# Decoding the second MLP's weights one matrix further ahead, with second buffers

## The chip, the cores and the metric

One core of a Trainium2 chip runs the whole program. The metric is the time of the device in microseconds for one execution, as a median over runs. The engines are TensorE (PE in the profile), VectorE (DVE), ScalarE (ACT), GpSimd (POOL), and SyncE (SP), which issues the DMAs. Each engine works through its own list of instructions strictly in order, so an instruction that waits holds up all that stands behind it on its engine.

## The reference

```python
def _moe_ref(x, w_gate, w_val, w_out):
    gate = 1.0 / (1.0 + np.exp(-(x @ w_gate)))
    val = x @ w_val
    return (gate * val @ w_out).astype(np.float32)

def _moe2_ref(x, w_a, w_b, w_out):
    a = x @ w_a
    b = x @ w_b
    return (a * b @ w_out).astype(np.float32)

def reference(**kwargs):
    attn_out = _attn_ref(**attn_kwargs)      # 4 x 8 heads, 576 positions, 64 wide, window of 64
    B, H, S, D = attn_out.shape
    x = np.ascontiguousarray(attn_out.transpose(0, 2, 1, 3)).reshape(B * S, H * D)
    x = _moe_ref(x=x, **moe_kwargs)
    return _moe2_ref(x=x, **moe2_kwargs)
```

The 2304 tokens are 512 wide. Both MLPs have 1536 hidden columns, and all six weight matrices arrive as 64-bit floats.

## The kernel before

The hidden columns of each MLP are cut into 12 chunks of 128 (NF = 12). The code counts the chunks of both MLPs in one row: F = 0 to 11 is the first MLP, F = 12 to 23 the second. A chunk has three matrices of 128 x 512 elements, a, b and o. Each is **decoded** on the chip, since the engines know no 64-bit floats: a matrix comes in as two 32-bit words for each element (tile st_a, st_b or st_o, by DMA), and becomes a high part and a low part for PE.

Decoding one matrix has two halves. decode_words (L371) builds the words: ACT makes low (L375) and ex (L378), DVE makes wi in two instructions (L381, L384), and POOL adds low to wi (L388). decode_pair (L392 on) is the split: DVE multiplies ex by wi (L394), ACT writes the high part (L400), and the low part is a subtraction (L403) that runs on DVE for a and b and on POOL for the second MLP's o. SP then saves the pair to DRAM (tiles ka, kb, ko). For the second MLP there are besides four sums and differences of halves of a and b, made by combinations: on POOL s (L447), on ACT the high part wq (L449), on POOL the low part of wq (L450), and a save by SP. There is one buffer for low, one for wi, two for ex.

In the second MLP, each chunk's up-projections are a **quad** (q0 to q11 below, one for each of F = 12 to 23): instead of eight block products seven are made, in the order 1, 5, 6, 2, 7, 4, 3, each of six matmuls, into three banks (qa, qb, qc). ACT copies intermediate sums out of a bank (r1, r2, r3, L845; pool "rs"), DVE adds them up (g0, g1 and qc, L848), multiplies (qa and qc, L858), ACT and DVE split the product into the hidden tile hh, hl (L477, L479), and PE multiplies that by the chunk's o into accq (L964). The result of the accumulation is added to resf (L968). While quad k is worked on, a later chunk is decoded, by calls of step_decode between pieces of PE's work. For the first MLP in this stretch the same is done with plain products (gps, vps, L468), with hr and hh made from them (L488, L477).

The order of instructions on each engine is fixed when the program is built: a scheduler, with its own cost model, places the work in the order in which the Python code emits it and as its buffers allow. In `decode`, one call of step_decode did one whole matrix, words and split together, and the loads of the next chunk came at the end of a chunk. In time: to about 225 us runs the attention with the first chunks of the first MLP, to 350 us the rest of it, from 350 to 560 us the quads of the second MLP's front blocks with the decoding of its chunks, from 640 us on all weights are fetched back ready-made from DRAM.

Of the kernel before, what the change touches and what calls it, by code (L numbers as in the profile page):

```python
# [21 lines left out]
def tile_window_attention_gated_mlps(ctx, tc, q, k, v, w1g, w1v, w1o, w2a, w2b, w2o, out):  # L22
# [348 lines left out]
    def decode_words(F, i, nm):  # L371
        st = staged.pop((F, nm))
        w0, w1 = st[:, :, 0], st[:, :, 1]
        low = dec.tile([P, DM], I32, tag="low", name="low")
        nc.scalar.activation(out=low, in_=w0.bitcast(U32), func=AF.Copy, scale=2.0 ** -29)  # L375
        yield
        ex = dec.tile([P, DM], F32, tag="ex", bufs=2, name="ex")
        nc.scalar.activation(out=ex, in_=w1.bitcast(F32), func=AF.Abs)  # L378
        yield
        wi = dec.tile([P, DM], I32, tag="wi", name="wi")  # L380
        nc.vector.tensor_scalar(  # L381
# [34 lines left out]

    def decode(F):
        for i, nm in enumerate("abo"):
            if nm not in parts.get(F, {}):
                whole(decode_words(F, i, nm))  # L420
                whole(decode_pair(F, i, nm))
                save(F, nm, pairs.pop((F, nm)))
                yield
                if F >= NF and nm == "b":
                    got = parts[F]
                    for n, t in combinations(got, full.pop((F, "a")), full.pop((F, "b"))):
                        nc.sync.dma_start(out=kept_q[F - NF][:, n], in_=t.bitcast(F32))
                    yield
        ready[F] = parts[F]

# [9 lines left out]
    def combinations(got, a, b):  # L440
# [3 lines left out]

        def combined(nm, x, y, op):
            s = late["sts"].tile([P, CH], F32, tag="s", name=f"s{nm}")
            nc.gpsimd.tensor_tensor(out=s, in0=x, in1=y, op=op)  # L447
            t = late["wq"].tile([P, 2, CH], F32R, tag="wq", name=f"wq{nm}")
            nc.scalar.activation(out=t[:, 0], in_=s, func=AF.Copy)  # L449
            nc.gpsimd.tensor_tensor(out=t[:, 1], in0=s, in1=t[:, 0].bitcast(F32), op=ALU.subtract)  # L450
            got[nm] = (t[:, 0], t[:, 1])
            return s, t

        s1, t5 = combined(5, b1, b2, ALU.add)
        s2, t6 = combined(6, s1, a1, ALU.subtract)
        _, t7 = combined(7, a1, b1, ALU.subtract)
        _, t3 = combined(3, a2, s2, ALU.subtract)
        return tuple(enumerate((t5, t6, t7, t3)))

# [182 lines left out]

    nload, ndec, dec_it, limit = [0], [0], [None], [NF - 1]

    def step_decode(turn):

        if dec_it[0] is None:
            F = ndec[0]
            if F >= NW or F > limit[0] or (F > G and last_use.get(F - G - 1, -1) >= turn):
                return False  # L650
            if nload[0] <= F:
                load_weights(F)
                nload[0] = F + 1
            dec_it[0] = decode(F)
            ndec[0] += 1
        if next(dec_it[0], "done") == "done":
            dec_it[0] = None
            F = ndec[0]
            if F < NW and nload[0] <= F:
                load_weights(F)  # L660
                nload[0] = F + 1
        return True
# [137 lines left out]
    def fetch(F, whole):  # L800
# [15 lines left out]
        else:  # L816
            f = got["f"].bitcast(F32)
            combinations(got, f[:, 0], f[:, 1])
        return got
# [220 lines left out]
    for F in range(DECODED):  # L1040
        ready[F] = parts[F]
    ndec[0] = nload[0] = DECODED
    done.update([*group_of, *BACK[:BEHIND]])

    for n, (group, fcs) in enumerate(plan):
# [6 lines left out]
        if n == SPAN.stop:  # L1052
# [3 lines left out]
            attend(steps=100)  # L1056
            next_part(early, (("op6", 1), ("hs", 1), ("wq", 8), ("sts", 3), ("rs", 3)), middle)
            limit[0] = NF + 1
# [246 lines left out]
```

## Time and profile before

| | us |
|---|---|
| median of 3 runs | 968.96 (966.82 to 969.8) |
| profiled execution, its own time | 969.65 |
| its span in the profile | 967.5 |
| PE busy | 931.7 (96%) |
| DVE busy | 687.1 (71%) |
| ACT busy | 482.1 (50%) |
| POOL busy | 360.4 (37%) |

The span is the stretch of the profiled execution from the first to the last instruction; 2.15 us of its time lie outside. Busy times are over the whole span, and the work isn't spread evenly: POOL has nothing to do in the last third, and 20 of every 25 us in some stretches of the second MLP's decoding. The mean clock granted to PE was 0.993 of full speed.

### The profile page before, as it was taken

The numbers are of one execution on the slowest core, as the hardware profiler recorded it, in microseconds if no ns is written. First come the engines' busy times: TensorE is split into PE (matmuls) and PEld (weight loads), VectorE is DVE, ScalarE is ACT, GpSimd is POOL, SyncE is SP. The second block draws the span as 40 slices with busy tenths as digits, with TensorE's granted clock in tenths as the row PEclk, the third lists the DMA queues.
The fourth block names the chain that finished last, engine by engine and source line by source line (L and its number), as shares of the span: only waits on it lengthen the run. The fifth ranks groups of instructions, "written<-read, shape, count | busy, mean of one in ns | idle before, by whom it ended". The sixth has DMA issues, their size and how long they took to land.

```text
span 967.5 us, 15682 instructions
## 1 busy us (share of the span) xinstructions
PE 931.7 (96%) x5504; PEld 776.6 (80%) x5504; DVE 687.1 (71%) x1339; ACT 482.1 (50%) x1063; POOL 360.4 (37%) x357
## 2 busy tenths in 40 slices
PE   7899999999799998998999998999999999999998
PEld 6798887887688886877887886788888888888886
DVE  6997877786653489878788866778888673344545
ACT  7887554576654365665556433664454233311111
POOL 4543223345422385686568518643440000000000
PEclk9999999999999999999999999999999999999999
DMA  8996698998763174767567547345455675554322
GB/s 212 246 246 194 215 342 305 314 302 269 249 210 110 70 249 149 254 231 248 196 214 261 210 150 262 111 159 169 141 174 197 217 255 159 164 172 129 101 66 87
DMA packets 146846, 193.69 MB, mean 200 GB/s; under 512 B 63825, under 2 KB 99153, under 8 KB 146769
## 3 DMA queue, kind: packets, MB, share of 16 engines
q1 hardware_dynamic: 146768, 192.71, 61.5%
q8 instruction: 43, 0.70, 0.3%
q14 instruction: 35, 0.28, 0.1%
HBM read 118.75 MB, written 69.47 MB: 195 GB/s over the span
## 4 chain that ended last, share of the span: by engine, by line
PE 68%; POOL 10%; DVE 9%; DMA 6%; issue 3%; ACT 3%; POOLq 0%; SPq 0%; DVEq 0%; ACTq 0%
PE qa L826 15%; PE accq L964 12%; PE qb L826 8%; PE gps L468 7%; PE vps L468 7%; PE accm L569 5%; PE qc L826 4%; POOL s L447 3%; POOL wi L388 3%; PE accy L927 3%; POOL wq L450 2%; PE accx L927 2%; DMA kf<-ex 2%; PE xps L228 2%; DMA wf<-kf 1%
## 5 line engine op out<-in xcount | busy, mean ns | idle before, releaser
L388 POOL TENSOR_TENSOR wi<-wi,low 128x512 int32<-128x512 int32 x72 | 101.8, 1413 | 136.3 <-DVE wi L384 99.3
L826 PE MATMUL qa<-op,wq 128*128 128x512 f32 x432 | 113.1, 390 | 1.5 <-ACT op L730 0.9
L826 PE MATMUL qb<-op,wq 128*128 128x512 f32 x432 | 111.5, 390 | 0.1
L468 PE MATMUL vps<-xh,wb 128*128 128x256 f32 (+1 forms) x392 | 106.9, 342 | 3.3 <-ACT hr L488 3.3
L845 ACT ACTIVATE r<-qa 128x512 f32<-128x512 f32 x108 | 62.6, 594 | 89.6 <-PE qa L826 88.1
L450 POOL TENSOR_TENSOR wq<-s,wq 128x256 fp32r<-128x256 f32 x96 | 88.4, 929 | 50.2 <-ACT wq L449 49.9
L468 PE MATMUL gps<-xh,wa 128*128 128x256 f32 (+1 forms) x392 | 105.7, 340 | 0.2 <-DVE hl L479 0.2
L826 PEld LDWEIGHTS qa<-op,wq 128*128 128x128 f32 x432 | 80.9, 188 | 19.4 <-ACT op L730 1.4
L826 PEld LDWEIGHTS qb<-op,wq 128*128 128x128 f32 x432 | 81.0, 188 | 17.4 <-DVE qc L848 0.5
L569 PE MATMUL accm<-hh,wo 128*128 128x512 f32 (+1 forms) x296 | 86.3, 359 | 4.2 <-DVE gacc L546 3.6
L394 DVE SCALAR_TENSOR_TENSOR ex<-ex,wi 128x512 f32<-128x512 f32 x72 | 58.2, 809 | 30.5 <-POOL wi L388 21.1
L468 PEld LDWEIGHTS vps<-xh,wb 128*128 128x128 f32 x392 | 70.8, 195 | 11.0 <-ACT hr L488 3.5
L468 PEld LDWEIGHTS gps<-xh,wa 128*128 128x128 f32 x392 | 70.0, 193 | 8.9 <-DVE hl L479 1.3
L964 PE MATMUL accq<-wo,h 128*128 128x512 f32 (+1 forms) x300 | 71.6, 382 | 1.8 <-DVE resf L968 1.7
L468 PE MATMUL gps<-xl,wa 128*128 128x256 f32 (+1 forms) x196 | 66.5, 339 | 0.6 <-DVE xl L237 0.6
L468 PE MATMUL vps<-xl,wb 128*128 128x256 f32 (+1 forms) x196 | 66.7, 340 | 0.0
L477 ACT ACTIVATE hh<-qa 128x512 fp32r<-128x512 f32 x36 | 21.5, 598 | 90.1 <-DVE qa L858 61.2
L964 PEld LDWEIGHTS accq<-wo,h 128*128 128x128 f32 x300 | 54.9, 188 | 13.6 <-DVE resf L968 2.3
L569 PEld LDWEIGHTS accm<-hh,wo 128*128 128x128 f32 x296 | 52.6, 189 | 13.5 <-DVE gacc L546 3.4
L964 PE MATMUL accq<-wo,hh 128*128 128x512 f32 x184 | 56.3, 397 | 5.8 <-ACT hh L477 5.6
L189 ACT ACTIVATE pr<-pr,stat 128x128 f32<-128x128 f32 x144 | 54.1, 391 | 12.3 <-DVE stat L183 11.9
L210 POOL TENSOR_TENSOR pr<-pr,stat 128x512 f32<-128x512 f32 x34 | 38.1, 1122 | 55.0 <-DVE stat L208 36.7
(177 smaller groups left out, 2125.7 us busy)
## 6 DMA issues: line engine op xcount, KB each, us to landing
wo<-ko SPq DMA_DIRECT2D x27, 512.0 KB, 4.1
wa<-ka SPq DMA_DIRECT2D x27, 512.0 KB, 4.4
st_o<-in_moe_w_out_dram SPq DMA_DIRECT2D x24, 512.0 KB, 5.0
ka<-wa SPq DMA_DIRECT2D x24, 512.0 KB, 4.9
kb<-wb SPq DMA_DIRECT2D x24, 512.0 KB, 4.6
ko<-wo SPq DMA_DIRECT2D x24, 512.0 KB, 4.3
kq<-wq SPq DMA_DIRECT2D x48, 256.0 KB, 3.5
wq<-kq SPq DMA_DIRECT2D x48, 256.0 KB, 3.1
```

The lines of the kernel that those rows point to most:

```text
L189: nc.scalar.activation(out=pr[e][:, j, :], in_=pr[e][:, j, :], func=AF.Exp, bias=nmax[:, e, j:j + 1], scale=-1.0, accum_out=None if t in O ...
L210: (nc.vector if t in OTHERS["norm"] else nc.gpsimd).tensor_tensor(out=pr[e], in0=pr[e], in1=den[:, e].unsqueeze(2).to_broadcast([P, NP, P] ...
L388: nc.gpsimd.tensor_tensor(out=wi, in0=wi, in1=low, op=ALU.add)
L394: nc.vector.scalar_tensor_tensor(out=wf, in0=wf, scalar=SMALLEST, in1=wi.bitcast(F32), op0=ALU.is_ge, op1=ALU.mult)
L447: nc.gpsimd.tensor_tensor(out=s, in0=x, in1=y, op=op)
L450: nc.gpsimd.tensor_tensor(out=t[:, 1], in0=s, in1=t[:, 0].bitcast(F32), op=ALU.subtract)
L468: nc.tensor.matmul(ps, lhsT=a[:, c * P:(c + 1) * P], rhs=b[:, c, :], start=(n == 0), stop=(n == 3 * NP - 1))
L569: nc.tensor.matmul(ps[:, m], lhsT=a[:, sl], rhs=b, start=k == 0, stop=k == total - 1)
L826: nc.tensor.matmul(ps, lhsT=a[:, c * P:(c + 1) * P], rhs=b[:, c, :], start=first and n == 0, stop=n == 5, skip_group_check=True,)
L845: nc.scalar.activation(out=r[n], in_=ps, func=AF.Copy)
L927: nc.tensor.matmul(bank[k], lhsT=a[n][i][:, sl], rhs=b[n][j], start=start and m == 0, stop=m == 2, skip_group_check=True,)
L964: nc.tensor.matmul(ps, lhsT=a, rhs=b, start=n == 0, stop=n == len(pairs) - 1)
```

## The change

The generator `decode`, which did matrix after matrix, goes. `begin_matrix` now issues the words of the next matrix and then at once the load of the same matrix of the next chunk, and step_decode does the split of the oldest matrix whose words are there. From F = 14 on (NF + 2) it first calls begin_matrix once more, so that the words of one further matrix stand ahead of the split. From F = 15 on, wi takes turns between its old buffer and a second one in a new pool "dec", and the ex of an o matrix gets a buffer of its own there, so that the two old ones are left to a and b. To make room, pool "rs" has two buffers instead of three. The four combinations of a chunk, once one step, are two steps of two; a first-MLP chunk takes three steps instead of four. What is computed and the number of instructions stay the same.

```diff
     def decode_words(F, i, nm):
         st = staged.pop((F, nm))
         w0, w1 = st[:, :, 0], st[:, :, 1]
+        k = 3 * F + i if F > NF + 2 else 0
         low = dec.tile([P, DM], I32, tag="low", name="low")
...
-        ex = dec.tile([P, DM], F32, tag="ex", bufs=2, name="ex")
+        ex = late["dec"].tile([P, DM], F32, tag="ex", name="ex") if k % 3 == 2 else dec.tile([P, DM], F32, tag="ex", bufs=2, name="ex")
...
-        wi = dec.tile([P, DM], I32, tag="wi", name="wi")
+        wi = (late["dec"] if k % 2 else dec).tile([P, DM], I32, tag="wi", name="wi")
...
-    def decode(F):
-        for i, nm in enumerate("abo"):
-            if nm not in parts.get(F, {}):
-                whole(decode_words(F, i, nm))
-                whole(decode_pair(F, i, nm))
-                save(F, nm, pairs.pop((F, nm)))
-                yield
-                if F >= NF and nm == "b":
-                    got = parts[F]
-                    for n, t in combinations(got, full.pop((F, "a")), full.pop((F, "b"))):
-                        nc.sync.dma_start(out=kept_q[F - NF][:, n], in_=t.bitcast(F32))
-                    yield
-        ready[F] = parts[F]
+    def combining(F):
+        got = combinations(parts[F], full.pop((F, "a")), full.pop((F, "b")))
+        for half in range(2):
+            for n, t in islice(got, 2):
+                nc.sync.dma_start(out=kept_q[F - NF][:, n], in_=t.bitcast(F32))
+            yield
...
+    def begin_matrix():
+        if begun[0] == 0:
+            load_weights(DECODED)
+        if begun[0] < len(order):
+            F, i, nm = m = order[begun[0]]
+            begun[0] += 1
+            whole(decode_words(*m))
+            pending.append(m)
+            if F + 1 < NW:
+                load_matrix(F + 1, nm)
 
     def step_decode(turn):
...
+        if combined_by:
+            if next(combined_by[0], combined_by) is not combined_by:
+                return True
+            combined_by.pop()
+        if not pending:
+            begin_matrix()
+        if not pending:
+            return False
+        F, i, nm = m = pending[0]
+        if F > limit[0] or (F > G and last_use.get(F - G - 1, -1) >= turn):
+            return False
+        if F >= NF + 2:
+            begin_matrix()
+        pending.pop(0)
+        whole(decode_pair(*m))
+        save(F, nm, pairs.pop((F, nm)))
+        if nm == "o":
+            ready[F] = parts[F]
+        elif nm == "b" and F >= NF:
+            combined_by.append(combining(F))
         return True
...
-            next_part(early, (("op6", 1), ("hs", 1), ("wq", 8), ("sts", 3), ("rs", 3)), middle)
+            next_part(early, (("op6", 1), ("hs", 1), ("wq", 8), ("sts", 3), ("rs", 2), ("dec", 1)), middle)
```

The order of instructions is the same on every engine up to about 225 us, and again once the front blocks' quads are done. Between, three places are shown. In the changed file the lines have moved by a few (L394 is L395 there, L848 is L861, L858 is L871, L388 is L389, L450 is L444, L447 is L441).

**ACT, in the last first-MLP chunks (about 262 us).** kt is a copy for the attention, ex and low are decoding words (ex_4355, now ex_4186, those of a later a matrix), hr is the copy of a product of the first MLP, which PE's next products in that bank wait for. Before:

```order
L118 ACTIVATE pt14_0_3498<-tps14_0_3493 128x512
L153 ACTIVATE kt17_3769<-kt16_3514 128x4x64
L378 ACTIVATE ex_4355<-st_a_4233 128x512
L488 ACTIVATE hr_3812<-gps_3786 128x256
L375 ACTIVATE low_4366<-st_b_4235 128x512
```

and now:

```order
L118 ACTIVATE kt16_3520<-kps16_3515 128x4x128
L401 ACTIVATE wo_3927<-ex_3918 128x512
L153 ACTIVATE kt17_3771<-kt16_3520 128x4x64
L483 ACTIVATE hr_3814<-gps_3788 128x256
L379 ACTIVATE ex_4186<-st_a_4033 128x512
L376 ACTIVATE low_4371<-st_b_4074 128x512
```

The copy hr, which stood behind the words ex, stands ahead of them.

**DVE, at quad q3 (about 430 to 438 us).** Here qc, qa and g belong to q3 (qa_5418 before, qa_5431 now, is the product that hh of q3 is split from); xacc is a sum of the accumulation's results; wi, ex and wb are decoding. Before, these stand behind the words of chunk 17's o matrix (wi_5513) and chunk 18's a (wi_5665):

```order
L403 TENSOR_TENSOR wb_5457<-ex_5450,wb_5457 128x512
L593 TENSOR_TENSOR xacc0_4918<-acc1_5384,xacc0_4918 128x512
L394 SCALAR_TENSOR_TENSOR ex_5511<-ex_5511,wi_5513 128x512
L381 TENSOR_SCALAR wi_5665<-st_a_5533 128x512
L384 SCALAR_TENSOR_TENSOR wi_5665<-st_a_5533,wi_5665 128x512
L858 TENSOR_TENSOR qa_5418<-qa_5418,g0_5416 128x512
L848 TENSOR_TENSOR g1_5417<-qb_5419,r2_5467 128x512
```

and now, with chunk 18's b (wi_5678) and o (wi_5707) and chunk 19's a (wi_5821):

```order
L385 SCALAR_TENSOR_TENSOR wi_5678<-st_b_5450,wi_5678 128x512
L588 TENSOR_TENSOR xacc0_4935<-acc0_5387,xacc0_4935 128x512
L588 TENSOR_TENSOR xacc0_4935<-acc1_5388,xacc0_4935 128x512
L395 SCALAR_TENSOR_TENSOR ex_5676<-ex_5676,wi_5678 128x512
L382 TENSOR_SCALAR wi_5821<-st_a_5545 128x512
L871 TENSOR_TENSOR qa_5431<-qa_5431,g0_5429 128x512
L385 SCALAR_TENSOR_TENSOR wi_5821<-st_a_5545,wi_5821 128x512
L404 TENSOR_TENSOR wb_5714<-ex_5676,wb_5714 128x512
L395 SCALAR_TENSOR_TENSOR ex_5705<-ex_5705,wi_5707 128x512
L861 TENSOR_TENSOR g1_5430<-qb_5432,r2_5484 128x512
```

The same product qa stands behind work for matrices that are two to three further on, and g1 behind three decoding instructions of its own.

**POOL, at the same quad.** The product qa of q3 above stands on DVE behind a multiplication L394 (now L395) that reads the wi which POOL adds up: wi_5513 before, wi_5678 now. POOL's rows up to that addition and on, before:

```order
L447 TENSOR_TENSOR s7_5479<-ex_5431,ex_5450 128x256
L450 TENSOR_TENSOR wq5_5471<-s5_5469,wq5_5471 128x256
L388 TENSOR_TENSOR wi_5513<-wi_5513,low_5509 128x512
L450 TENSOR_TENSOR wq6_5476<-s6_5474,wq6_5476 128x256
L450 TENSOR_TENSOR wq7_5481<-s7_5479,wq7_5481 128x256
L447 TENSOR_TENSOR s3_5484<-ex_5431,s6_5474 128x256
```

and now:

```order
L441 TENSOR_TENSOR s7_5514<-ex_5405,ex_5444 128x256
L441 TENSOR_TENSOR s3_5520<-ex_5405,s6_5492 128x256
L444 TENSOR_TENSOR wq6_5494<-s6_5492,wq6_5494 128x256
L404 TENSOR_TENSOR wo_5414<-ex_5291,wo_5414 128x512
L444 TENSOR_TENSOR wq7_5516<-s7_5514,wq7_5516 128x256
L404 TENSOR_TENSOR wo_5548<-ex_5465,wo_5548 128x512
L444 TENSOR_TENSOR wq3_5522<-s3_5520,wq3_5522 128x256
L389 TENSOR_TENSOR wi_5678<-wi_5678,low_5674 128x512
L389 TENSOR_TENSOR wi_5707<-wi_5707,low_5703 128x512
```

Before it was POOL's row number 186 of the whole program, now it is number 193: seven more of POOL's instructions (three wq, one s, one wo, two wi) stand ahead of it.

## Rows read from the trace of the kernel before

**Rows 1.** Windows: us; busy PE, PEld, DVE, ACT, POOL (instructions); clock, DMA, GB/s.

```profile
350.00:375.00 25.00, 22.12 (x109) 18.23 (x108) 24.46 (x32) 14.26 (x26) 14.71 (x12) 0.93 0.51 179
375.00:437.00 62.00, 57.03 (x266) 45.82 (x264) 49.51 (x70) 41.01 (x80) 50.47 (x46) 1.00 0.68 231
425.00:525.00 100.00, 94.82 (x425) 78.48 (x424) 82.12 (x124) 54.84 (x103) 69.16 (x66) 0.97 0.67 227
700.00:725.00 25.00, 25.00 (x112) 20.63 (x111) 20.87 (x34) 12.37 (x25) 10.34 (x14) 1.00 0.55 178
```

**Rows 2.** ACT's timeline, 255 to 270 us.

```profile
262.19 0.40 ACT L153 ACTIVATE kt<-kt 128x256 f32<-128x256 f32 x1
264.19 0.67 ACT L378 ACTIVATE ex<-st_a 128x512 f32<-128x512 f32 x1 [1.60 <-DVE wo L403]
264.77 0.37 ACT L488 ACTIVATE hr<-gps 128x256 f32<-128x256 f32 x1
```

**Rows 3.** PE's timeline, 257 to 272 us.

```profile
265.19 0.58 PE L468 MATMUL vps<-xh,wb 128*128 128x256 f32 x1 [3.29 <-ACT hr L488]
```

**Rows 4.** PE's timeline, 366 to 384 us.

```profile
378.83 1.43 PE L826 MATMUL qa<-op,wb 128*128 128x512 f32 x5 [0.47 <-DVE op L736]
```

**Rows 5.** DVE's timeline, 429 to 444 us.

```profile
430.16 0.68 DVE L403 TENSOR_TENSOR wb<-ex,wb 128x512 fp32r<-128x512 f32 x1
...
433.42 1.22 DVE L394 SCALAR_TENSOR_TENSOR ex<-ex,wi 128x512 f32<-128x512 f32 x1 [1.98 <-POOL wi L388]
...
436.56 0.68 DVE L858 TENSOR_TENSOR qa<-qa,g 128x512 f32<-128x512 f32 x1
```

**Rows 6.** PE's timeline, 429 to 445 us.

```profile
433.76 1.07 PE L826 MATMUL qa<-op,wq 128*128 128x512 f32 x4
437.93 1.20 PE L964 MATMUL accq<-wo,hh 128*128 128x512 f32 x4 [3.11 <-ACT hh L477]
```

**Rows 7.** Chain of waits, 400 to 800 us: start, length, engine, group.

```profile
439.13 2.40 PE gps L468 x12
...
443.95 1.42 PE gps L468 x12
...
449.56 1.36 PE accq L964 x6
...
510.46 2.60 PE accq L964 x6
```

**Rows 8.** DVE's timeline, 503 to 516 us.

```profile
504.89 0.69 DVE L394 SCALAR_TENSOR_TENSOR ex<-ex,wi 128x512 f32<-128x512 f32 x1 [0.27 <-POOL wi L388]
...
508.25 0.69 DVE L858 TENSOR_TENSOR qa<-qa,g 128x512 f32<-128x512 f32 x1
```

**Rows 9.** PE's timeline, 503 to 516 us.

```profile
510.46 1.75 PE L964 MATMUL accq<-wo,hh 128*128 128x512 f32 x4 [1.87 <-ACT hh L477]
```

**Rows 10.** Groups by form, 335 to 600 us, POOL.

```profile
L450 POOL TENSOR_TENSOR wq<-s,wq 128x256 fp32r<-128x256 f32 x58 | 56.4, 986 | 2.2 <-ACT wq L449 2.1
L388 POOL TENSOR_TENSOR wi<-wi,low 128x512 int32<-128x512 int32 x33 | 47.1, 1429 | 38.6 <-DVE wi L384 36.2 <-ACT hr L492 2.3
...
L403 POOL TENSOR_TENSOR wo<-ex,wo 128x512 fp32r<-128x512 f32 x12 | 18.7, 1561 | 10.7 <-ACT wo L400 10.7
```

**Rows 11.** Waits that end in 375 to 437 us: total, times, longest.

```profile
POOL wi L388 <- DVE wi L384: 15.6, 3, 9.5
...
POOL s L447 <- DVE ex L394: 3.2, 4, 0.8
```

**Rows 12.** ACT's timeline, 520 to 533 us.

```profile
526.23 0.59 ACT L845 ACTIVATE r<-qa 128x512 f32<-128x512 f32 x1
```

**Rows 13.** DVE's timeline, 522 to 533 us.

```profile
529.75 0.68 DVE L848 TENSOR_TENSOR g<-qb,r 128x512 f32<-128x512 f32 x1
```

**Rows 14.** POOL's timeline, 410 to 416 us.

```profile
412.70 1.25 POOL L447 TENSOR_TENSOR s<-s,ex 128x256 f32<-128x256 f32 x1
```

**Rows 15.** DVE's timeline, 410 to 416 us.

```profile
413.28 1.23 DVE L403 TENSOR_TENSOR wb<-ex,wb 128x512 fp32r<-128x512 f32 x1
```

More of the change, by code (lines that the diff above doesn't have):

```diff
@@ L443, in combinations, with combined @@
         (a1, a2), (b1, b2) = ((f[:, 0:CH], f[:, CH:]) for f in (a, b))
-        def combined(nm, x, y, op):
+        def combined(n, nm, x, y, op):
             s = late["sts"].tile([P, CH], F32, tag="s", name=f"s{nm}")
@@ L451, in combined @@
             got[nm] = (t[:, 0], t[:, 1])
[L452 to L458, printed above, removed]
+            return s, (n, t)
+        s1, t = combined(0, 5, b1, b2, ALU.add)
+        yield t
+        s2, t = combined(1, 6, s1, a1, ALU.subtract)
+        yield t
+        yield combined(2, 7, a1, b1, ALU.subtract)[1]
+        yield combined(3, 3, a2, s2, ALU.subtract)[1]
     def product(ps, w, x):
@@ L641, in tile_window_attention_gated_mlps @@
     NW = 2 * NF
-    nload, ndec, dec_it, limit = [0], [0], [None], [NF - 1]
-    def step_decode(turn):
[L647 to L661, printed above, removed]
+    limit = [NF - 1]
+    order = [(F, i, nm) for F in range(DECODED, NW) for i, nm in enumerate("abo")]
+    begun, pending, combined_by = [0], [], []
+    def begin_matrix():
[8 more added lines that the diff above has]
+                load_matrix(F + 1, nm)
+    def step_decode(turn):
+        if combined_by:
[18 more added lines that the diff above has]
+            combined_by.append(combining(F))
         return True
@@ L817, in fetch @@
             f = got["f"].bitcast(F32)
-            combinations(got, f[:, 0], f[:, 1])
+            *_, = combinations(got, f[:, 0], f[:, 1])
         return got
@@ L1041, in tile_window_attention_gated_mlps @@
         ready[F] = parts[F]
-    ndec[0] = nload[0] = DECODED
     done.update([*group_of, *BACK[:BEHIND]])
```

## The prediction

> **What bounds the kernel now.** I read the windows first, to see which engine is full in which stage. From 640 us on PE is: 25.00 us busy of 25, at full clock, in 700 to 725 [rows 1]. All of the decoding is over by then, so nothing that this change does can shorten that part; it only starts earlier or later. The change has to earn its time between 225 and 560 us. There PE is nearly full too, 57.03 of 62 us from 375 to 437 and 94.82 of 100 us from 425 to 525 [rows 1]. So about 5 us can be won in each of these stretches at the most, and only where PE stands still. I went from there to PE's timeline and looked for its longest idle times and what ended them. Three are large enough to matter: 3.29 us before 265.19, which the copy hr on ACT ended [rows 3], 3.11 us before 437.93 and 1.87 us before 510.46, both ended by hh of a quad on ACT [rows 6, 9]. Last I followed each of the three back on the engine that was late, with the timelines of ACT and DVE, and set beside it what stands there in the changed order.
>
> The sum goes against the profiled execution's own 969.65 us. The median of the runs is 0.7 us lower, and I take that off at the end.
>
> **ACT at 262 us.** The kt copy ends at 262.59. Behind it stood the words ex<-st_a, which waited until 264.19 for a buffer, and only behind these the hr that PE waited for, at 264.77 [rows 2]. With hr ahead of ex it can start at 262.59, since the product it copies was finished before PE went idle at 261.90 (265.19 less 3.29). That is 264.77 - 262.59 = **2.2 us** won. The ex that is moved back loses nothing, as its buffer came free only at 264.19. Neither end is far: 0 if PE's head start is lost in the next stretch, where DVE is busy 24.46 of 25 us [rows 1], and 3.3 if the matmuls behind the gap keep their speed too.
>
> **DVE between 363 and 380 us.** Here DVE is the full engine, and the order now puts one pair of word instructions of chunk 15 in front of the differences that q0's operand op is made from. PE already waits 0.47 us for such an op at 378.83 [rows 4]. Such a pair takes at most 1.9 us, the time between L394's end at 434.64 and qa's start at 436.56, with POOL busy beside it [rows 5]. It lies between 0 and 1.9; I take **1.0 us lost**.
>
> **DVE and POOL at quad q3.** PE is done with q3's products at 434.83, and hh is late by 3.11 us [rows 6]. It is late since qa (L858) starts on DVE only at 436.56, behind L394, L381 and L384 of the decoding, and L394 had stood 1.98 us waiting for POOL's addition [rows 5]. In the changed order qa stands behind L395 and L382, one instruction less, which by these rows lets POOL's addition end 1.1 to 2.0 us later without harm (3.14 us from L394's start to qa's before; 1.22 us and a word instruction now). But the addition that L395 needs is seven POOL instructions later. By their means these are three wq at 0.99, one s taken like a wq, one wo at 1.56 and two wi at 1.43, 8.4 us [rows 10]. So POOL has to do 6.4 to 7.3 us of work in time in which it used to stand, only for qa to be where it was. It has that time: 62 - 50.47 = 11.5 us idle from 375 to 437 [rows 1]. Of this, 6.1 us (15.6 less the 9.5 that lie before 375) it waited for DVE's wi, and 3.2 us for ex [rows 11]. These are the two waits that words one step ahead and a second wi take away, 9.3 us together. That leaves 9.3 - 6.4 = 2.9 down to 9.3 - 7.3 = 2.0 us by which qa comes earlier; I take **2.5 us** of the 3.11. What is late next is the same qa, by 0.6 us.
>
> With PE's idle time goes slow running behind it: twelve gps take 2.40 us right after the wait and 1.42 us five us later [rows 7], 1.0 us more, at a lower granted clock. With most of the wait gone I count **0.8 us** of that.
>
> **DVE at quad q7.** The same picture at 508.25: qa stands behind an L394 that began at 504.89 and three more decoding instructions, 3.4 us in all [rows 8], and PE waits 1.87 us for hh [rows 9]. The six accq behind take 2.60 us where six take 1.36 elsewhere [rows 7]. The work is the same at each quad, and by q7 the decoding has had four more chunks to get ahead, so I count both, 1.8 and 1.2, **3.0 us**.
>
> **Buffers "rs", two for three.** r1 and r3 now share a buffer, and r2 of the next quad has to wait until g1 of this one is added. In the trace r2 of a quad starts at 526.23, and the g1 that would have to be done first ends at 530.43, 4.2 us later [rows 12, 13], the largest such lag I found. PE needs r2 copied before product 7; what lies between is product 2 at least, six matmuls like the six of 1.36 us [rows 7], at the most two sums of accq of the same length besides. So 0.1 to 2.8 us at a quad can stand open, and the order has g1 behind three decoding instructions. I take the middle at one quad, **1.4 us lost**.
>
> **The rest costs nothing that I can find.** The loads st move ahead of some saves on SP, and start earlier than before; the words are needed no sooner than before. Steps of three instead of four in the first MLP move decoding earlier, into a stretch where the gap at 262 us is the largest. The combinations in two halves are the same instructions.
>
> The sum: -2.2 + 1.0 - 2.5 - 0.8 - 3.0 + 1.4 = -6.1, so 963.5 us on the profiled execution's scale and **962.8** as a median.
>
> **A rule that speaks against it.** POOL's s at 412.70 took 1.25 us and DVE's wb at 413.28 took 1.23 us [rows 14, 15], while the same wb takes 0.68 us at 430.16 [rows 5]: the two engines hold each other up. The Trainium skill says why ("SBUF — State Buffer", section "SBUF: two separate sides"): GpSimd shares a pair of ports with VectorE's operations that read two SBUF inputs, and whoever has it has it for its whole instruction. The trace agrees, 1.23 being 0.68 and most of another instruction. By that rule part of POOL's idle time is not there to be had, and the sum would be that of the second rival, 966.4.
>
> **Rivals.**
>
> *POOL can't make good the seven instructions (slower).* The mechanism is the in-order queue of DVE: qa waits behind L395, L395 for POOL. For it speaks that POOL is already the busiest of the three helpers there, 50.47 of 62 us [rows 1]; against it that 9.3 us of its idle time have just the causes that are taken away [rows 11]. If none of the idle time is recovered, qa is 6.4 us later instead of 2.5 earlier, nothing comes back at q7 either, and the sum is -2.2 + 1.0 + 6.4 + 1.4 = +6.6, or 976 us. It decides when POOL recovers less than about 6 of its 11.5 us: then q3 gives nothing back; below 4 us it costs 2.4 or more and eats the gain at 262 us.
>
> *DVE and POOL in each other's way (no change).* A chunk takes 18.1 us (510.46 - 437.93 over four quads) [rows 6, 9]. DVE's decoding instructions with two inputs are eight in it, at 0.68 us 5.4 us, 30 us in the 100 from 425 to 525, and POOL is busy 69.16 [rows 1, 5]: 99 of 100 us, if none of POOL's busy time is waiting. Some of it is, as at 412.70. Then only a third of the 8.3 us at q3 and q7 comes back and the sum is -2.2 + 1.0 - 2.8 + 1.4 = -2.6, 966.4 us as a median.
>
> *The ring of two.* If four quads stand open by 2.1 us each, it costs 8.4 for 1.4 us: -6.1 + 7.0 = +0.9, about 970 us.
>
> **How the numbers follow.** A measurement of this kernel can tell 0.3%, 2.9 us, from no change. I give the forecast 0.56, with its own range of 958 to 966: down to -3.3 - 3.1 - 1.0 - 3.0 = -10.4 where nothing is lost and the clock is kept, up to -3. The slow POOL has 0.16, the two engines in each other's way 0.18, the ring 0.10. Most of the forecast and some of the second rival are faster: 0.57. The rest of that rival and most of the ring are the same: 0.24. The slow POOL and the worst of the ring are slower: 0.19. The range from 955 to 971.5 leaves out the worse half of the slow POOL and little else; its lower end is the -10.4 less the 2.9 us that PE stands idle from 350 to 375 [rows 1], which I counted at nothing.
>
> **What would show it.** Right: hr on ACT directly after kt at about 262.6; PE's wait for hh at q3 under 1 us, and none at q7; POOL's waits for DVE's wi gone from 375 to 437 and its busy time there near 60 of 62 us. Wrong: DVE's L395 waiting for POOL with a qa behind it, for several us; PE waiting for r at product 7 of many quads; a new wait of PE between 365 and 380 for op.

## The result: 977.0 us for 968.7, slower by 0.75%

The changed kernel took 977.01 us (median of 4 runs, 975.53 to 977.40), the kernel before beside it 968.67 us. The ratio is 1.0075, with a 95% interval of 1.0052 to 1.0098: slower, by 8.3 us. The prediction was 962.8 us, in a range of 955 to 971.5.

The head of the page of the profile after:

```profile
span 974.8 us, 15689 instructions
...
PE 931.6 (96%) x5504; PEld 774.5 (79%) x5504; DVE 701.3 (72%) x1339; ACT 480.8 (49%) x1063; POOL 358.9 (37%) x357
```

PE did the same work in the same busy time (931.7 us before), and the span is 7.3 us longer: PE stands still for longer. DVE is busy 14.2 us longer than before (687.1) with the same 1339 instructions. POOL is not (360.4 before). So DVE's own instructions have become slower. The windows, with the columns of [rows 1]:

```profile
350.00:375.00 25.00, 21.42 (x110) 17.23 (x111) 24.39 (x31) 14.40 (x25) 13.83 (x10) 1.00 0.46 161
375.00:437.00 62.00, 54.08 (x246) 43.12 (x244) 56.04 (x69) 41.83 (x81) 54.23 (x48) 0.97 0.74 248
425.00:525.00 100.00, 93.55 (x421) 76.01 (x419) 86.26 (x118) 54.34 (x104) 66.44 (x65) 0.98 0.66 223
700.00:725.00 25.00, 25.00 (x112) 20.62 (x111) 21.28 (x35) 12.19 (x24) 10.73 (x15) 1.00 0.59 189
```

From 375 to 437 us DVE is busy 56.04 us where it was 49.51, with one instruction fewer, and PE 54.08 where it was 57.03 [rows 1]. The back part is as before, PE full.

PE's 5504 matmuls are the same in both kernels, so the place of the loss can be read from rows at which PE has the same amount of work behind it (starts in us):

| PE's row | before | after | later by |
|---|---|---|---|
| vps<-xl,wb | 340.17 | 338.92 | -1.25 |
| qa<-op,wb, at q0 | 378.83 | 378.45 | -0.38 |
| gps<-xh,wa, ahead of q2 | 401.83 | 407.01 | 5.18 |
| qa<-op,wb, at q3 | 429.22 | 434.39 | 5.17 |
| vps<-xl,wb, behind q3 | 442.72 | 448.07 | 5.35 |
| qa<-op,wa | 450.76 | 457.72 | 6.96 |
| qa<-op,wa, ahead of q7's hh | 494.78 | 504.06 | 9.28 |
| qb<-op,wq, behind q7's hh | 514.91 | 520.38 | 5.47 |
| qa<-op,wb | 521.73 | 528.89 | 7.16 |
| accq<-wo,hh | 563.40 | 570.73 | 7.33 |

Up to q0 the changed kernel is ahead. Between 378 and 407 us it loses 5.6 us, and never makes them good. PE's timeline there, with the idle time before a row and what ended it in brackets (compare [rows 4]); first before:

```profile
380.10 1.53 PE L826 MATMUL qa<-op,wq 128*128 128x512 f32 x6
381.73 1.67 PE L826 MATMUL qb<-op,wq 128*128 128x512 f32 x6
```

and after:

```profile
378.45 1.42 PE L839 MATMUL qa<-op,wb 128*128 128x512 f32 x5 [0.48 <-DVE op L749]
381.34 1.65 PE L839 MATMUL qb<-op,wq 128*128 128x512 f32 x6 [1.46 <-DVE qc L861]
382.83 1.52 PE L839 MATMUL qa<-op,wq 128*128 128x512 f32 x6
...
394.79 1.65 PE L839 MATMUL qb<-op,wq 128*128 128x512 f32 x6 [1.05 <-DVE qc L861]
...
399.70 0.39 PE L463 MATMUL gps<-xh,wa 128*128 128x256 f32 x1 [1.90 <-DVE g L861]
...
403.13 2.13 PE L839 MATMUL qa<-op,wq 128*128 128x512 f32 x6
```

Three new waits, of 1.46, 1.05 and 1.90 us, are for sums of the quads on DVE (qc, g), which stand in its queue among the decoding. The first of these sums is not late: it starts at 380.60, where it started at 380.99 before. But PE now has the product that needs it (qb) ahead of one that does not (qa), where it stood behind. In all, PE is idle 3.9 us longer between the two rows than before. The other 1.7 us are slow matmuls behind the waits: the granted clock is 0.66 of full from 400 to 405 us, where it was 1.00, so for part of that time it was at the lower of its two levels, 1.2 GHz. Six matmuls take 2.13 us there, where six take 1.52 elsewhere. The window, with the columns of [rows 1]:

```profile
400.00:405.00 5.00, 5.00 (x22) 4.24 (x21) 5.00 (x8) 3.26 (x7) 5.00 (x5) 0.66 0.96 337
```

DVE's own rows of that stretch show what became denser. From the start of q1's g<-qc,r to that of q2's, the kernel before takes 16.54 us (386.77 to 403.31) and does 11 decoding instructions, 8.9 us by their durations. The changed one takes 24.85 us (385.22 to 410.07) and does 19, for 20.3 us, without a pause. At 0.41 us for L382 and 0.68 us for the others, the durations of undisturbed rows, the 11 would take 6.7 us and the 19 would take 11.6. So this stretch holds some 4.9 us more of decoding work, and 6.4 us more by which instructions are longer. From q0's g to q11's it is 107 decoding instructions in both kernels: the work is not more, it is bunched. The rows ahead of the sum that PE waits for at 394.79:

```profile
391.30 0.68 DVE L404 TENSOR_TENSOR wa<-ex,wa 128x512 fp32r<-128x512 f32 x1
391.90 1.77 DVE L395 SCALAR_TENSOR_TENSOR ex<-ex,wi 128x512 f32<-128x512 f32 x1
393.70 0.43 DVE L382 TENSOR_SCALAR wi<-st_a 128x512 int32<-128x512 int32 x1
394.04 0.69 DVE L861 TENSOR_TENSOR qc<-qb,r 128x512 f32<-128x512 f32 x1
```

### The profile page after: what moved, and what is told of

Its sections match the earlier page's. It is cut to its first block, busy times and chain, and to the rows that moved or that the text cites. A ratio compares the mean times of both kernels' runs of the same rounds, so it can differ in the third digit from the quotient of the medians.

```text
span 974.8 us, 15689 instructions
## 1 busy us (share of the span) xinstructions
PE 931.6 (96%) x5504; PEld 774.5 (79%) x5504; DVE 701.3 (72%) x1339; ACT 480.8 (49%) x1063; POOL 358.9 (37%) x357
## 4 chain that ended last, share of the span: by engine, by line
PE 49%; DVE 12%; DMA 4%; POOL 4%; issue 3%; ACT 3%; SPq 0%; POOLq 0%; DVEq 0%; ACTq 0%
PE qa L839 14%; PE accq L977 10%; PE qb L839 7%; PE qc L839 3%; PE gps L463 3%; PE accy L940 3%; PE vps L463 3%; DVE wi L385 2%; PE accx L940 2%; DVE ex L395 2%; DVE wi L382 2%; POOL wi L389 1%; DMA st_o<-in_moe_w_out_dram 1%; PE accm L564 1%; DMA st_a<-in_moe_w_a_dram 1%
## 5 line engine op out<-in xcount | busy, mean ns | idle before, releaser
L389 POOL TENSOR_TENSOR wi<-wi,low 128x512 int32<-128x512 int32 x72 | 104.0, 1444 | 118.7 <-DVE wi L385 81.6
L858 ACT ACTIVATE r<-qa 128x512 f32<-128x512 f32 x108 | 63.4, 595 | 117.2 <-PE qa L839 97.2
L444 POOL TENSOR_TENSOR wq<-s,wq 128x256 fp32r<-128x256 f32 x96 | 86.5, 907 | 73.1 <-ACT wq L443 71.2
L463 PE MATMUL vps<-xh,wb 128*128 128x256 f32 (+1 forms) x392 | 104.9, 336 | 1.2 <-ACT hr L483 1.2
L395 DVE SCALAR_TENSOR_TENSOR ex<-ex,wi 128x512 f32<-128x512 f32 x72 | 65.1, 906 | 16.4 <-ACT ex L379 7.7
L564 PEld LDWEIGHTS accm<-hh,wo 128*128 128x128 f32 x296 | 52.5, 189 | 12.1 <-ACT hh L472 1.5
L839 PE MATMUL qa<-op,wb 128*128 128x512 f32 x216 | 55.7, 392 | 3.2 <-ACT r L858 2.7
```

The lines of the kernel that those rows point to most:

```text
L389: nc.gpsimd.tensor_tensor(out=wi, in0=wi, in1=low, op=ALU.add)
L395: nc.vector.scalar_tensor_tensor(out=wf, in0=wf, scalar=SMALLEST, in1=wi.bitcast(F32), op0=ALU.is_ge, op1=ALU.mult)
L463: nc.tensor.matmul(ps, lhsT=a[:, c * P:(c + 1) * P], rhs=b[:, c, :], start=(n == 0), stop=(n == 3 * NP - 1))
L564: nc.tensor.matmul(ps[:, m], lhsT=a[:, sl], rhs=b, start=k == 0, stop=k == total - 1)
L839: nc.tensor.matmul(ps, lhsT=a[:, c * P:(c + 1) * P], rhs=b[:, c, :], start=first and n == 0, stop=n == 5, skip_group_check=True,)
L858: nc.scalar.activation(out=r[n], in_=ps, func=AF.Copy)
```

## The experiments

Each was timed beside the kernel before on the same chip; medians and ratios are against that.

**Words ahead, taken away.**

```diff
-        if F >= NF + 2:
-            begin_matrix()
```

> The changed kernel without the call that begins one more matrix from F = 14 on, so that words and split of a matrix stand together again; the second buffers, the ring of two, the earlier loads, the halved combinations and the three steps of a first-MLP chunk stay. Theory A, words ahead make DVE and POOL work at the same time and slow DVE's instructions on SBUF (DVE busy 701 against 687 us, loss all in q1 and q2): 965 to 969 us, DVE busy back to about 687. Theory B, the ring of two for r: stays near 976. Theory C, the earlier decoding in the first MLP: stays near 976.

Measured: 976.08 us against 969.38, ratio 1.0078 (1.0052 to 1.0103), DVE busy 700.5. This is the number of theories B and C; theory A, for which the run was made, missed it. The early call is not what costs: theory A had the right symptom with the wrong part of the edit.

**The ring of three for r, given back.**

```diff
-            next_part(early, (..., ("rs", 2), ("dec", 1)), middle)
+            next_part(early, (..., ("rs", 3), ("dec", 1)), middle)
...
-        ex = late["dec"].tile(...) if k % 3 == 2 else dec.tile([P, DM], F32, tag="ex", bufs=2, name="ex")
+        ex = dec.tile([P, DM], F32, tag="ex", bufs=2, name="ex")
```

> The changed kernel with three buffers for r again; the second buffer for ex of an o matrix is given up for the space. Theory A: DVE busy stays about 700 and the time 973 to 978. Theory B: back to 966 to 970, with PE's and DVE's waits for r and g gone.

Measured: 979.35 us against 969.38, ratio 1.0094 (1.0059 to 1.0130), DVE busy 698.7. This is on theory A's side, 1.4 us above its range, and far from theory B's.

**The ring of two alone, on the kernel before.**

```diff
-            next_part(early, (..., ("rs", 3)), middle)
+            next_part(early, (..., ("rs", 2)), middle)
```

> The kernel before with two buffers for r in the second MLP's front quads in place of three, nothing else. Theory A: within 2 us of before, 967 to 971. Theory B: 974 to 978.

Measured: 967.37 us against 969.38, ratio 0.9973 (0.9950 to 0.9997). The smaller ring costs nothing; if anything it gains 2 us. Theory B is out.

**All the buffers, without the new order of emission, on the kernel before.**

```diff
+        k = 3 * F + i if F > NF + 2 else 0
...
-        ex = dec.tile([P, DM], F32, tag="ex", bufs=2, name="ex")
+        ex = late["dec"].tile(...) if k % 3 == 2 else dec.tile([P, DM], F32, tag="ex", bufs=2, name="ex")
...
-        wi = dec.tile([P, DM], I32, tag="wi", name="wi")
+        wi = (late["dec"] if k % 2 else dec).tile([P, DM], I32, tag="wi", name="wi")
...
-            next_part(early, (..., ("rs", 3)), middle)
+            next_part(early, (..., ("rs", 2), ("dec", 1)), middle)
```

> The kernel before with all of the buffers of the changed one (two for wi in turns, a third for ex of o, two for r) and the old order of emission, in which words and split of a matrix stand together. Theory A: the scheduler can pull little ahead without the words being issued early, so 967 to 971, DVE busy under 692. Theory B: 974 to 978 for the ring.

Measured: 977.28 us against 969.38, ratio 1.0089 (1.0062 to 1.0116). This is the whole loss, with the old order of emission. Theory A missed it. It is the number that theory B had, but the run before this one had put the ring out; what is left of the edit is the second wi and the third ex. Its window from 375 to 437 us is nearly that of the changed kernel:

```profile
375.00:437.00 62.00, 54.23 (x246) 43.20 (x244) 56.02 (x69) 41.96 (x81) 54.41 (x48) 0.97 0.73 247
```

So the loss does not need the early call. Which of the two buffers brings it, and what the scheduler does with it, the next two runs show.

**Which buffer: the second wi, or the third ex.** Two runs, each the kernel before with one of the two, and three buffers for r.

```diff
+        k = 3 * F + i if F > NF + 2 else 0
...
-        wi = dec.tile([P, DM], I32, tag="wi", name="wi")
+        wi = (late["dec"] if k % 2 else dec).tile([P, DM], I32, tag="wi", name="wi")
...
-            next_part(early, (..., ("rs", 3)), middle)
+            next_part(early, (..., ("rs", 3), ("dec", 1)), middle)
```

The second run has the changed kernel's line for ex in place of that for wi.

> The kernel before with a second buffer for wi alone, in turns from F = 15 on; three buffers for r, two for ex as before. The buffers alone had given 977 us. Theory D, wi is the one: with a second wi DVE no longer stands waiting for POOL's addition, the two engines run at once and slow each other: 974 to 979, DVE busy about 698. Theory E, it is the third ex: within 2 us of before.

> The kernel before with a buffer of its own for the ex of o matrices from F = 15 on, one wi, three buffers for r. Theory D: 966 to 971, DVE busy about 688. Theory E: 974 to 979.

Measured: with the second wi 978.55 us against 969.45, ratio 1.0106 (1.0072 to 1.0141), DVE busy 697.4; with the third ex 971.40, ratio 1.0025 (1.0004 to 1.0046), DVE busy 686.5, 0.4 us above theory D's range. The second wi carries the loss; the third ex may cost some 2 us. The scheduler places instructions by what their buffers allow: given a second wi, it pulls decoding ahead by itself. Between the starts of q1's and q2's g<-qc,r the first run has 16 decoding instructions on DVE, where the kernel before has 11, and the order of emission is the same.

**All but the second buffers.** The changed kernel with k and both late buffers gone, first with two and then with three buffers for r.

```diff
-        k = 3 * F + i if F > NF + 2 else 0
...
-        ex = late["dec"].tile(...) if k % 3 == 2 else dec.tile([P, DM], F32, tag="ex", bufs=2, name="ex")
+        ex = dec.tile([P, DM], F32, tag="ex", bufs=2, name="ex")
...
-        wi = (late["dec"] if k % 2 else dec).tile([P, DM], I32, tag="wi", name="wi")
+        wi = dec.tile([P, DM], I32, tag="wi", name="wi")
...
-            next_part(early, (..., ("rs", 2), ("dec", 1)), middle)
+            next_part(early, (..., ("rs", 2)), middle)
```

> The changed kernel without its second buffers for wi and ex; words one step ahead, loads, halved combinations, three steps and the ring of two stay. If the buffers carry the loss and the order of emission does nothing by itself: 964 to 969, near the ring of two alone (967.4). If the order of emission carries a loss of its own: 973 or more.

> The changed kernel without second buffers and with three buffers for r: the order of emission alone. If it is worth something without the ring of two: 964 to 967. If the 3 us of the run without second buffers came from the ring: 968 to 971.

Measured: with two buffers for r 966.44 us against 969.45, ratio 0.9972 (0.9954 to 0.9991); with three 964.75 us against 967.31, ratio 0.9963 (0.9944 to 0.9982). Both are faster than either kernel of this case. The order of emission, with earlier loads and three steps for a chunk of the first MLP, is worth some 3 us by itself, with or without the ring. With that theory C is out too: the earlier decoding in the first MLP is in both of these runs.

**DVE beside POOL, measured by itself.**

```python
for _ in range(16): nc.vector.tensor_scalar(out=wi, in0=w1, scalar1=3, scalar2=(1 << 30) - 1, ...)
for _ in range(16): nc.vector.scalar_tensor_tensor(out=ex, in0=g, scalar=SMALLEST, in1=wi.bitcast(F32), ...)
for _ in range(16): nc.vector.tensor_tensor(out=res, in0=qa, in1=g, op=ALU.mult)      # qa in PSUM
```

> No MLP at all: a small program in which DVE runs 16 times each of three forms, the word instruction (tensor_scalar, 128x512 integers), the multiplication ex by wi (two inputs from SBUF) and a multiplication with one input from PSUM, first with POOL idle and then while POOL runs 48 additions of 128x512 integers. If DVE and POOL hold each other up at SBUF: 0.42, 0.69 and 0.69 us alone; beside POOL about 1.2 us or more for the first two, each up to one POOL instruction later, and 0.69 for the third. If the longer means in the large kernel have another cause (DMA, PE): the same times in both halves.

DVE's timeline, start and length of each group of 16, first with POOL idle and then beside it:

```profile
4.05 7.36 DVE L40 TENSOR_SCALAR wi<-src 128x512 int32<-128x512 int32 x16 [1.58 <-DMA src<-in_moe_w_out_dram]
11.45 11.59 DVE L44 SCALAR_TENSOR_TENSOR ex<-g,wi 128x512 f32<-128x512 f32 x16
22.96 11.56 DVE L48 TENSOR_TENSOR res<-qa,g 128x512 f32<-128x512 f32 x16
...
34.77 21.47 DVE L40 TENSOR_SCALAR wi<-src 128x512 int32<-128x512 int32 x16
56.27 26.64 DVE L44 SCALAR_TENSOR_TENSOR ex<-g,wi 128x512 f32<-128x512 f32 x16
82.83 11.55 DVE L48 TENSOR_TENSOR res<-qa,g 128x512 f32<-128x512 f32 x16
```

and POOL's 48 additions:

```profile
34.93 70.55 POOL L54 TENSOR_TENSOR add<-add,low 128x512 int32<-128x512 int32 x48 [34.49 <-DVE add L52]
```

Per instruction (length over 16): the word instruction takes 0.46 us alone and 1.34 beside POOL, the multiplication 0.72 and 1.67, the one that reads PSUM 0.72 and 0.72. The first two touch only SBUF. PE does nothing in this program and no DMA runs during these groups, so POOL alone is enough to make them about as long as they get in the kernel. The Trainium skill's page "SBUF — State Buffer" (section "SBUF: two separate sides") has the rule, that the loser of the shared ports waits for the winner's whole instruction. The trace agrees in kind, not in size: with POOL's addition at 1.26 us (the last seven, after DVE was done) the rule would make 1.26 + 0.46 = 1.72 and 1.26 + 0.72 = 1.98 us, and 1.34 and 1.67 were measured.

**The same orders with less of POOL's work.** In the finished programs, so that no instruction changes its place, POOL's additions of low to wi are cut from 512 to 32 columns; the words of the other columns lack the addition.

```python
block.instructions[at] = copy.replace(ins, outs=[narrow(a) for a in ins.outs], ins=[narrow(a) for a in ins.ins])
```

> The kernel before in its own order of instructions, with POOL's addition of low to wi cut from 512 to 32 columns in the finished program, so that the words of the other columns lack it. It is the measure for the next run: POOL holds DVE up less and DVE waits less for POOL. By every theory somewhat faster than before, 955 to 967.

> The changed kernel in its own order, POOL's additions cut in the same way. Theory A, the loss is DVE and POOL holding each other up: with a third of POOL's work gone the distance to the run before it shrinks from 8 us to 4 or less, and DVE's busy time falls by more here than there. Theory F, the loss is the place of the decoding ahead of the quads in DVE's queue, whatever it takes: the distance stays 7 to 10 us.

Measured: 952.65 us for the order of before, 953.64 for the changed one. The first is 2 us below the range that I gave it. The distance shrinks from 8.3 to 1.0 us, and DVE's busy time falls by 9.2 us to 677.9 in the one and by 21.9 us to 679.4 in the other. Both are as theory A has it, and theory F, which gives the whole loss to the place in the queue, is out.

The distance of the whole times says too much, though. In the two traces the changed order is already 5.3 us ahead at q0 (PE's row qa<-op,wb at 370.16 for 375.42), where it was 0.4 ahead with whole additions, and from there to about 545 us it loses 3.8 us of that (543.78 for 545.24). With whole additions it loses 8.6 us over the same stretch (-0.38 at q0, 550.33 for 542.13 at its end). So 3.8 of 8.6 us stay when POOL's additions are short. That part is with the order, of which theory F had a piece. From q1's g<-qc,r to q2's DVE still has 19 decoding instructions where the other order has 11, and takes 20.89 us for 14.74. These are single executions, the slowest of four of the one order and the fastest of four of the other, so the lead at q0 is rather too large.

**The same orders with less of DVE's work.** POOL's additions are whole; the multiplication of ex by wi is cut to 32 columns in the same way, and leaves out the other columns.

> The kernel before in its own order, with DVE's multiplication of ex by wi cut from 512 to 32 columns in the finished program (the other columns of the weights stay wrong); POOL's work is whole. The measure for the next run. DVE waits for POOL here as long as before, so a faster DVE gains little: 958 to 967.

> The changed kernel in its own order with the same cut. If the loss is that DVE is full, with its instructions lengthened beside POOL, the cut of about 34 us of DVE's work between 350 and 566 us takes most of it away, with POOL's chain as long as ever: within 4 us of the run before it. If the short additions had helped only because POOL's chain became shorter: still 7 us or more behind it.

Measured: 954.68 and 959.48 us. The distance is 4.8 us, between the two forecasts, which alone would leave it open; the kernel before gained 14.6 us, more than I expected of it. The group of the cut instruction in the second run (instructions, busy us, mean ns) says why:

```profile
L395 DVE SCALAR_TENSOR_TENSOR ex<-ex,wi 128x32 f32<-128x32 f32 x31 | 17.7, 573 | 7.0 <-ACT ex L379 3.6 <-POOL wi L389 3.5
```

A multiplication of 32 columns still takes 573 ns on the mean, and in the first run 407. The first run's rows show two levels, 0.19 us and some 0.72:

```profile
389.64 0.19 DVE L394 SCALAR_TENSOR_TENSOR ex<-ex,wi 128x32 f32<-128x32 f32 x1 [1.18 <-POOL wi L388]
395.11 0.71 DVE L394 SCALAR_TENSOR_TENSOR ex<-ex,wi 128x32 f32<-128x32 f32 x1
```

Of the 72 multiplications of that run, the 52 beside which POOL did nothing took at most 0.19 us. Most of those beside POOL took 0.69 to 0.73. So the time that the cut leaves is POOL's, and this run takes away less of DVE's excess than I meant. By PE's rows the changed order is 3.3 us ahead at q0 here (371.52 for 374.82) and 5.0 behind at the end (533.68 for 528.67): it loses 8.3 us in the stretch, nearly the 8.6 of the whole kernels. The 4.8 us of distance are that loss less the earlier lead.

**The words ahead, and the second buffers, from F = 18 on.**

```diff
-        k = 3 * F + i if F > NF + 2 else 0
+        k = 3 * F + i if F > NF + 6 else 0
...
-        if F >= NF + 2:
+        if F >= NF + 6:
             begin_matrix()
```

> The changed kernel with words ahead from F = 18 and second buffers from F = 19 on, in place of 14 and 15; the ring of two stays. Theory G, the loss comes only where DVE is already full, in q0 to q2 (363 to 410 us): 964 to 969. Theory A without that condition: most of the loss is still there, 972 to 977.

Measured: 975.10 us against 967.31, ratio 1.0067 (1.0046 to 1.0087). Theory G falls. By the starts of g<-qc,r, this kernel is 1.1 us ahead of before at q4; at q5 it is 3.5 and at q6 5.2 us behind. The loss has moved with the place where the second wi comes in:

```profile
400.00:425.00 25.00, 25.00 (x123) 21.19 (x122) 18.06 (x29) 17.28 (x35) 18.18 (x17) 1.00 0.71 244
475.00:500.00 25.00, 20.16 (x83) 14.64 (x81) 24.44 (x32) 13.17 (x26) 22.84 (x21) 1.00 0.77 252
```

From 475 to 500 us DVE is busy 24.44 of 25 us and PE 20.16, where the kernel before has 20.35 and 24.79; from 400 to 425, behind the place where the changed kernel had lost, PE is full. It needs no stretch in which DVE is full already; the decoding that gets ahead fills it.

## Why the prediction was wrong

**ACT at 262 us: right in its mechanism, smaller in its sum.** ACT's timeline has hr right behind kt:

```profile
262.52 0.41 ACT L153 ACTIVATE kt<-kt 128x256 f32<-128x256 f32 x1
262.82 0.37 ACT L483 ACTIVATE hr<-gps 128x256 f32<-128x256 f32 x1
```

hr starts at 262.82, 1.95 us earlier than before [rows 2], and PE's wait for it falls from 3.29 us [rows 3] to 1.25:

```profile
255.70 0.66 PE L142 MATMUL kps<-ident,k 128*128 128x128 f32 x4 [2.10 <-DVE stat L183]
...
263.24 0.39 PE L463 MATMUL vps<-xh,wb 128*128 128x256 f32 x1 [1.25 <-ACT hr L483]
...
267.65 0.50 PE L463 MATMUL gps<-xh,wa 128*128 128x512 f32 x1 [1.60 <-DVE hl L474]
```

But two waits have taken part of it, 2.10 us for the attention's stat on DVE and 1.60 for hl. What was left in the next stretch, at 340 us, is 1.25 us, for 2.2 in the sum.

**DVE between 363 and 380 us: right.** DVE's g of q0 starts 1.31 us earlier than before, at 366.84 for 368.15. Behind it stand the two word instructions that are new there, and the next multiplication starts only 0.38 us earlier, at 375.58 for 375.96:

```profile
368.10 0.41 DVE L382 TENSOR_SCALAR wi<-st_a 128x512 int32<-128x512 int32 x1
...
371.64 0.68 DVE L385 SCALAR_TENSOR_TENSOR wi<-st_a,wi 128x512 int32<-128x512 int32 x1
...
375.58 0.69 DVE L395 SCALAR_TENSOR_TENSOR ex<-ex,wi 128x512 f32<-128x512 f32 x1 [1.19 <-POOL wi L389]
```

That is 0.9 us lost, for 1.0 in the sum, and with it most of the head start was gone. PE's lead there falls to 0.38 us too.

**DVE and POOL at quad q3: this is the step that failed.** I wrote that the waits "that words one step ahead and a second wi take away" are "9.3 us together", and took them as time in which POOL works and qa comes 2.5 us earlier. The waits did go. But PE, 5.17 us behind at 429 us, is 5.35 us behind once q3's products are done: 0.2 us lost, for 2.5 + 0.8 won in the sum. And the sum has no term at all for the 5.6 us that PE loses from 378 to 407 us, where the same waits are gone. POOL's waits, from 375 to 437 us:

```profile
POOL wi L389 <- DVE wi L385: 11.7, 2, 10.4
...
POOL s L441 <- DVE ex L395: 2.1, 3, 0.8
```

Of the 11.7 us, 10.4 are one wait that began ahead of the stretch and had its counterpart in the 9.5 of before, so 1.3 are left of 6.1; and 2.1 of 3.2 [rows 11]. hh of q3 and q7 no longer keeps PE waiting, either. POOL's busy time in the stretch grew by 3.8 us, to 54.23, where I had put it near 60. But POOL working in that time means POOL working beside DVE. DVE's groups by form from 350 to 560 us before (busy us and mean ns, then idle time before it and for whom):

```profile
L394 DVE SCALAR_TENSOR_TENSOR ex<-ex,wi 128x512 f32<-128x512 f32 x31 | 27.5, 888 | 19.7 <-POOL wi L388 15.0 <-ACT resf L966 1.9 <-ACT hr L492 1.4
...
L848 DVE TENSOR_TENSOR g<-qc,r 128x512 f32<-128x512 f32 x12 | 8.1, 678 | 0.0
...
L384 DVE SCALAR_TENSOR_TENSOR wi<-st_b,wi 128x512 int32<-128x512 int32 x10 | 6.8, 682 | 0.1
...
L381 DVE TENSOR_SCALAR wi<-st_b 128x512 int32<-128x512 int32 x10 | 4.2, 418 | 0.1
```

and after:

```profile
L395 DVE SCALAR_TENSOR_TENSOR ex<-ex,wi 128x512 f32<-128x512 f32 x31 | 33.9, 1097 | 5.8 <-ACT ex L379 3.6 <-POOL wi L389 1.6 <-ACT hh L472 0.7
...
L385 DVE SCALAR_TENSOR_TENSOR wi<-st_b,wi 128x512 int32<-128x512 int32 x10 | 8.9, 889 | 0.1
...
L861 DVE TENSOR_TENSOR g<-qc,r 128x512 f32<-128x512 f32 x11 | 7.5, 678 | 1.3 <-PE qc L839 1.3
...
L382 DVE TENSOR_SCALAR wi<-st_b 128x512 int32<-128x512 int32 x10 | 7.2, 719 | 0.0
```

DVE's idle time ahead of the multiplication for POOL's addition goes from 15.0 to 1.6 us, and the multiplication itself from 888 to 1097 ns. Of the b matrices one word instruction goes from 418 to 719, the other from 682 to 889; other groups grow less, and wb<-ex,wb goes from 1024 to 1001. g, which reads PSUM, stays at 678. Over the nine groups of the decoding on DVE (three each of the two word instructions, the multiplication, two subtractions) the busy time goes from 90.7 to 106.5 us. The wait for POOL has become part of the instructions: 13.4 us less of the one, 15.8 us more of the other. The difference is where it stands. With one wi the decoding went at the pace of that buffer. Without it, it runs as fast as both engines go, and in the quads where it gets ahead DVE is busy almost without a break, with eight more decoding instructions between the sums of q1 and q2. The second and the third of the three sums above start 3.4 and 0.7 us later than before (394.04 for 390.60, 398.97 for 398.27).

At q3 a new wait takes the place of the one for hh. DVE stands for a load, and behind it, in DVE's queue, stands the sum that PE needs:

```profile
434.80 1.03 DVE L382 TENSOR_SCALAR wi<-st_o 128x512 int32<-128x512 int32 x1 [1.44 <-DMA st_o<-in_moe_w_out_dram]
435.75 0.94 DVE L382 TENSOR_SCALAR wi<-st_b 128x512 int32<-128x512 int32 x1
436.62 0.68 DVE L385 SCALAR_TENSOR_TENSOR wi<-st_o,wi 128x512 int32<-128x512 int32 x1
437.22 0.69 DVE L861 TENSOR_TENSOR qc<-qb,r 128x512 f32<-128x512 f32 x1
```

PE's row behind it waited 2.05 us and then ran slowly, six matmuls in 2.49 us:

```profile
437.96 2.49 PE L839 MATMUL qb<-op,wq 128*128 128x512 f32 x6 [2.05 <-DVE qc L861]
```

How much of the loss is the lengthening, and how much the order? The runs with a second wi have 7 to 16 us more of these nine groups than the kernel before, and are 7 to 10 us slower; those without have -1 to 3 us more, and lie between 3 us faster and 2 us slower. Within the first kind the two do not go together: with second buffers from F = 19 on it is 98.0 us, 7.3 more, for 7.8 us of time. The pairs in which both kernels were cut alike, with PE's loss from q0 on as worked out above:

| run against its reference | DVE's decoding, us | time, us | PE's loss from q0 to about 540 us |
|---|---|---|---|
| changed kernel, kernel before | 106.5, 90.7: +15.8 | +8.3 | 8.6 |
| short multiplications, changed and before | 88.3, 76.2: +12.1 | +4.8 | 8.3 |
| short additions, changed and before | 86.9, 87.4: -0.5 | +1.0 | 3.8 |

That the second wi causes the loss, and that DVE and POOL hold each other up at SBUF, is shown. Of the way from the one to the other, this much is: where the lengthening stays, the loss stays; where it goes, 4.8 of the 8.6 us go with it. The other 3.8 us come without it, from the order that the scheduler makes with the second buffer, on DVE and, at 381 us, on PE itself. Cutting POOL's additions also shortens the chain of additions, so that the 4.8 us are all the lengthening's own is not shown.

**The rivals.** The one on the slow side had 976 us, close to the measured time, but not by its mechanism: that is luck. Ahead of the addition that q3's L395 needs, at 438.57, POOL had stood 2.16 us waiting for DVE's words; it was not POOL that was late. A part of the right mechanism stood in the second rival and in the rule, and its price was wrong. I let it take part of the gain away (966.4 us) and left every DVE instruction at its mean of before. The rows had what was needed: 1.23 us beside POOL for 0.68 [rows 5, 15], which is 0.55 us more, and so less than half of POOL's 1.25. That rival's 8.3 us at q3 and q7 are besides 7.2 by its own rows (3.11 + 1.0 and 1.87 + 1.2); it would have said 966.8.

**DVE at q7: won, and then lost again.** The wait for hh is gone there. PE is 9.28 us behind ahead of it and 5.47 behind it, 3.8 us won for the 3.0 of the sum. But at 526.03 PE waits 1.41 us for resf on DVE, and is 7.16 behind.

In the kernel with the order of emission alone both waits are still there (bracket: idle time and releaser), and by the two ratios it is some 11 us faster than the changed one:

```profile
436.22 1.64 PE L976 MATMUL accq<-wo,hh 128*128 128x512 f32 x4 [3.06 <-ACT hh L471]
```

```profile
508.12 1.19 PE L976 MATMUL accq<-wo,hh 128*128 128x512 f32 x4 [1.26 <-ACT hh L471]
```

PE waits 3.06 and 1.26 us for hh there. The gaps that I meant to close cost less than closing them this way.

**The ring of two: wrong in sign.** 1.4 us lost in the sum; -2.0 us measured alone. **The loads: not nothing.** I wrote that "the words are needed no sooner than before". With a second wi they are: DVE waits for no load between 350 and 560 us in the kernel before, and 3.3 us for st_o in the changed one. 1.44 us of these stand ahead of the sum that PE waits for at 437.96, as shown above. With the second wi alone, on the kernel before, DVE has no such wait there, and the loss is as large; so it is not the cause of the whole.

## What to carry to other kernels

A buffer that makes a producer wait for its consumer also keeps the two from running at once. Where both work in SBUF and one of them is GpSimd and the other VectorE, taking the wait away lengthened the instructions of both here, so price a filled idle time at the durations that the trace shows beside the other engine, not at the means. And where a scheduler places the work, a buffer alone can move more than the order of the code: test the buffers by themselves first, and count what now stands in the queue ahead of the instructions that the full engine waits for. When two cut programs are compared, compare them over the stretch in question: the distance of the whole times holds every earlier lead as well.

## What the runs showed of the hardware

In the small program a DVE instruction that touches SBUF alone grows by about 0.9 us beside GpSimd's 128x512 additions, the short one as much as the long one (0.46 to 1.34, 0.72 to 1.67 us), and one with an input in PSUM does not grow (0.72 and 0.72). In the kernel with short multiplications the growth is mostly 0.5 us, and again not a matter of DVE's columns: 128x32 takes 0.19 us with GpSimd idle and mostly 0.72 beside it. GpSimd pays less: in the small program its addition took 1.33 us beside the word instruction, 1.57 beside the multiplication, 1.30 beside the instruction on PSUM and 1.26 alone. So the pair is not wholly one after the other: some 0.3 to 0.4 us of each DVE instruction still ran beside POOL's (1.72 less 1.34, 1.98 less 1.67).
